# Loading a band of bias factors by DMA, loading a first q, k pair unpacked, and one DVE reordering, in a fused attention and maxout kernel

## The chip, the cores and the metric

The kernel runs on one core of one Trainium2 chip. The metric is the device time of one execution in microseconds (us); less is better. Engines are named as in the profile: PE is TensorE, ACT ScalarE, DVE VectorE, POOL GpSimd, SP SyncE. POOL, SP and ACT also issue DMAs.

## The reference

Inputs are q, k, v of shape (8, 8, 576, 64) (batch, heads, sequence, head dimension), a bias table of 32 buckets by 8 heads and four weight matrices, all float32. Cut to what matters:

```python
scores = q @ k.transpose(0, 1, 3, 2) / sqrt(D)
n = abs(pos[:, None] - pos[None, :])
scores += bias_table[bucket(n)].transpose(2, 0, 1)[None]   # constant for n >= 128 or so
attn = softmax(scores)                                     # over the keys
x = (attn @ v).transpose(0, 2, 1, 3).reshape(B * S, H * D) # 4608 tokens x 512
h = maximum(maximum(x @ w1, x @ w2), x @ w3)               # 768 wide
out = h @ w_out                                            # 4608 x 512, float32
```

## The kernel before, in words

Everything is computed in bf16 with float32 accumulation. The work goes batch by batch, and inside a batch by four pairs of heads (`hp` 0 to 3). For a pair PE makes transposed scores (keys on partitions, queries along the row), ACT takes their exponential into a tile `e4` for the first 512 keys and a tile `el` for the 64 left-over keys, PE multiplies by v with a column of ones behind it, and DVE divides by the row sums (`reciprocal`, then a product: the quotients, L962 and L963) into `x_sb`. Then `x_sb` is transposed into `xT` and fed to the three projections, of which chunks of 512 tokens (256 at the start) are laid between the attention work so that PE always has something to do.

The bias is not added to the scores. Its exponential, less a constant, is a factor that differs from 1 only in a band of 384 around the diagonal. `spread_bias` builds one row of 511 factors for each head and stores it to DRAM as `w_dr`. Two DMAs on SP's queue (`load_hank`, L340) read it back as `hank`: partition p holds the row shifted by p, 384 wide, 128x4x384 for each half of the heads. DVE multiplies the exponentials by reversed slices of `hank`: `times_band` (L807), `times_band_pair` (L822), `times_band_left` (L920). The left-over keys of a pair lie stacked, 64 partitions for each head, so they need another layout: `bandt`, 128 x 4 pairs x 192. In the kernel before, POOL makes it from `hank` with two reversing copies of 64x768 (`make_bandt`, L356), and `times_bandt` (L907) multiplies `el` by it.

Batch 0 (called batch one in the words of the change) is done in two passes. The first pass (loop at L1100) makes the scores of the first 256 queries of all four pairs, and at `hp` 3 DVE multiplies the bands of pairs 0 and 1. The second pass (loop at L1132) makes the other queries and meanwhile the first half of the values: at `hp` 0 the quotients of pair 0, then `bands(2)` (the bands of the third pair's first half), then the quotients of pair 1, then `bands(3)`; the copy of a transposed piece of q to `qT` (L126) comes behind. At `hp` 1 PE turns `x_sb` of pair 1 into `xT` (`x_transposes(1, 0)`, tiles `xp`), begins with the second half of the values, and so on. The second half of a pair's values (`attend(0, hp, e4, el, 1)`) reads the part of `el` that `times_bandt` writes.

Between the passes, `load_second` (L1072) puts on POOL's queue everything that batch 1 needs. q and k of batch 1 come packed: a partition takes four consecutive rows of a head, so that a run in DRAM and in the tile is long (`load_packed`, L247). They land in spare columns of `xT` and are spread into the tiles `q_sb`, `k_sb` (where the heads alternate) by `spread_packed` (L252): pair 0 by POOL, pairs 1 to 3 later by DVE. PE then transposes these (`second_transposes`, L781).

What sets the order: each engine runs its instructions in the order of the program (`inorder`). A DMA counts as an instruction of the engine that issues it, and POOL, SP and ACT issue in order too. DMAs of POOL use eight semaphores in turn (DMASW0 to DMASW7), so that one more DMA waits until the DMA eight before it has landed; DMAs of SP do the same with DMAHW0 to DMAHW7. `go_behind(loads, ins)` makes a load wait for an instruction `ins`. `divided[0, 0, 0]` is the second instruction (L963) of pair 0's first quotients. Tiles in PSUM come from pools with two buffers each (`ps_a` for the values, `ps_f` for transposes and projections, `ps_s` for scores).

## Time and profile before

| what | value |
|---|---|
| time, median of 3 runs | 308.22 us (306.51 to 308.97) |
| time of the profiled execution | 307.46 us |
| its span in the trace | 305.7 us |
| PE, DVE, ACT, POOL busy | 294.5, 206.9, 201.3, 143.7 us (96, 68, 66, 47%) |
| granted TensorE clock | 1.0 throughout |
| DMA, mean over the span | 133 GB/s in 165777 packets |

The span runs from the first to the last instruction; the time of the execution has 1.8 us around it. A row of the timeline gives the start, the length, the engine, the line, the operation with output <- inputs and, in brackets, how long the engine was idle before it and what ended that. Rows of the DMA view give the bytes of one DMA and the median time from its issue to its landing. A row of the DMA queues gives packets, MB and the time of the packets as a share of 16 DMA engines. Tile names in the profile have no numbers; in the order of instructions they do.

### The profile page before, as it was taken

To read this page: it belongs to the slowest core of one execution; us is meant where nothing else is said; L and a number is where in the kernel's file an instruction comes from. 1 tells how busy PE (TensorE), PEld (TensorE's weight loads), DVE (VectorE), ACT (ScalarE), POOL (GpSimd) and SP (SyncE) were. 2 spreads that over 40 slices of the span, in tenths; PEclk is the share of its full clock that TensorE was granted. 3 is DMA by queue.
4 is the path that set the end of the run, shared out by engine and by line. 5 is a ranking of instruction groups with operands and counts; after the bars stand their busy time and mean duration, and the time that the engine had idled before them with its cause. 6 is when DMAs were issued, how large, how long until landed. Compare 5 with 4: busy or idle time off the path is not lost.

```text
span 305.7 us, 10992 instructions
## 1 busy us (share of the span) xinstructions
PE 294.5 (96%) x4736; PEld 183.6 (60%) x4745; DVE 206.9 (68%) x455; ACT 201.3 (66%) x270; POOL 143.7 (47%) x199
## 2 busy tenths in 40 slices
PE   8778999999999999999999999999999999999995
PEld 2356878775556576667666766676667654444442
DVE  6489688787767767776777677767776765453552
ACT  3997998987786677768776877677777720222211
POOL 8998786725739655865686669460000000000000
PEclk9999999999999999999999999999999999999999
DMA  9999999999999999999999999999543013202003
GB/s 158 195 197 194 177 144 144 98 163 122 217 152 129 147 197 168 161 133 200 152 159 127 192 180 146 128 197 153 49 84 135 11 36 91 90 0 105 35 0 137
DMA packets 165777, 40.51 MB, mean 133 GB/s; under 512 B 154585, under 2 KB 161249, under 8 KB 165729
## 3 DMA queue, kind: packets, MB, share of 16 engines
q0 software_dynamic: 105664, 16.66, 96.6%
q1 hardware_dynamic: 58304, 22.69, 40.8%
q8 instruction: 37, 0.61, 0.9%
q10 hardware_dynamic: 1760, 0.47, 0.7%
q14 instruction: 12, 0.09, 0.2%
HBM read 35.39 MB, written 9.45 MB: 147 GB/s over the span
## 4 chain that ended last, share of the span: by engine, by line
PE 87%; ACT 6%; DVE 4%; issue 1%; DMA 1%; DVEq 0%; ACTq 0%
PE psp L109 36%; PE ps L109 17%; PE a L109 14%; PE sc L109 9%; PE pso L109 6%; ACT e L827 4%; PE sct L109 2%; PE warm L109 1%; PE scq L109 1%; DVE e L807 1%; ACT el L827 1%; DVE qT L126 1%; DMA out_dram<-osb 1%; DVE e L822 1%; PE tp L113 1%
## 5 line engine op out<-in xcount | busy, mean ns | idle before, releaser
L827 ACT ACTIVATE e<-sc 128x1024 bf16<-128x1024 f32 x128 | 129.0, 1026 | 29.6 <-PE sc L109 28.3
L109 PEld LDWEIGHTS <-w_bf 64*128 64x128 bf16 (+1 forms) x1112 | 75.9, 95 | 55.1 <-issue 1.5
L109 PE MATMUL psp<-xT,w_bf 64*128 64x512 bf16 x784 | 97.2, 376 | 0.0
L807 DVE TENSOR_TENSOR e<-e,hank 128x512 bf16<-128x512 bf16 (+2 forms) x120 | 57.7, 486 | 13.9 <-ACT e L827 13.2
L109 PE MATMUL ps<-xT,w_bf 128*128 128x512 bf16 (+1 forms) x324 | 58.9, 332 | 0.3
L109 PE MATMUL sc<-qT,kT 64*128 64x256 bf16 (+1 forms) x352 | 48.6, 319 | 2.4 <-ACT e L827 1.1
L199 POOL DMA_DIRECT2D k_sb<-in_k_dram x48 | 36.2, 768 | 18.3 <-DMA vx<-in_v_dram 10.6
L109 PE MATMUL a<-vx,e 64*128 64x65 bf16 (+1 forms) x1664 | 44.7, 190 | 0.0
L109 PEld LDWEIGHTS <-kT 64*128 64x128 bf16 (+1 forms) x712 | 30.1, 94 | 24.2 <-issue 7.1
L109 PEld LDWEIGHTS <-e 64*128 64x128 bf16 (+1 forms) x1664 | 40.7, 95 | 4.2
L199 POOL DMA_DIRECT2D q_sb<-in_q_dram x48 | 36.5, 771 | 11.9 <-DMA k_sb<-in_k_dram 3.0
L109 PEld LDWEIGHTS <-hT 64*128 64x128 bf16 (+1 forms) x462 | 28.2, 95 | 18.7 <-DVE hT L551 1.6
L167 POOL DMA_DIRECT2D vx<-in_v_dram x28 | 24.9, 899 | 23.0 <-DMA vx<-in_v_dram 9.3
L109 PE MATMUL psp<-wo_bf,hT 64*128 64x256 bf16 (+1 forms) x360 | 31.7, 305 | 0.0
L421 ACT ACTIVATE m<-ps 128x512 bf16<-128x512 f32 x14 | 8.4, 597 | 34.3 <-PE ps L109 34.3
L109 PEld LDWEIGHTS <-el 64*128 64x128 bf16 (+1 forms) x676 | 26.4, 94 | 7.0 <-issue 4.4
L827 ACT ACTIVATE el<-sct 128x576 bf16<-128x576 f32 (+2 forms) x36 | 21.7, 605 | 13.1 <-PE sct L109 13.0
L109 PE MATMUL a<-vt,el 64*128 64x65 bf16 (+1 forms) x260 | 29.6, 198 | 0.2 <-DVE m L511 0.2
L551 DVE TENSOR_TENSOR hT<-psp,m 128x1024 bf16<-128x1024 f32 (+1 forms) x20 | 18.7, 956 | 8.2 <-PE psp L109 8.2
L109 PE MATMUL pso<-wo_bf,hT 128*128 128x512 bf16 (+2 forms) x98 | 21.2, 366 | 0.2
L430 DVE TENSOR_TENSOR m<-ps,m 128x512 bf16<-128x512 f32 x14 | 9.7, 692 | 17.0 <-PE ps L109 17.0
L537 DVE TENSOR_TENSOR m<-psp,m 128x1024 bf16<-128x1024 f32 x15 | 18.4, 1224 | 3.3 <-PE psp L109 3.1
(82 smaller groups left out, 291.7 us busy)
## 6 DMA issues: line engine op xcount, KB each, us to landing
out_dram<-osb SPq DMA_DIRECT2D x35, 256.0 KB, 4.1
vx<-in_v_dram POOLq DMA_DIRECT2D x28, 128.0 KB, 6.3
q_sb<-in_q_dram POOLq DMA_DIRECT2D x50, 64.0 KB, 5.0
k_sb<-in_k_dram POOLq DMA_DIRECT2D x48, 64.0 KB, 4.8
w_bf<-in_moe_w_dram POOLq DMA_DIRECT2D x2, 512.0 KB, 8.5
xT<-in_k_dram SPq DMA_DIRECT2D x6, 128.0 KB, 4.6
hank<-w_dr SPq DMA_DIRECT2D x2, 384.0 KB, 4.8
w_bf<-in_moe_w_dram POOLq DMA_DIRECT2D x1, 768.0 KB, 8.4
```

The costliest lines, as they stand in the source:

```text
L109: made = inorder(nc.tensor.matmul(*args, **kw))
L113: inorder(nc.tensor.transpose(*args))
L126: return inorder(nc.vector.tensor_copy(out_, in_))
L167: in_turn(b, nc.gpsimd.dma_start(out=dst[:, t, h0:h1, :], in_=x[:, t, h0:h1, :]), P * (h1 - h0))
L199: in_turn(b, nc.gpsimd.dma_start(out=dst[:, g, :, par, :], in_=part), KT * P)
L421: nc.scalar.activation(out=st[fb]["m0"][:], in_=ps0, func=ACTF.Copy)
L430: inorder(nc.vector.tensor_tensor(out=m[:], in0=ps1, in1=st[fb]["m0"][:], op=ALU.max))
L537: return lambda: inorder(nc.vector.tensor_tensor(out=m[0][:], in0=ps1(), in1=m[0][:], op=ALU.max,))
L551: inorder(nc.vector.tensor_tensor(out=out_[:, i : i + n], in0=ps2()[:, i : i + n], in1=m[0][:, i : i + n], op=ALU.max,))
L807: put(nc.vector.tensor_tensor(out=e4[:, t, :, lo:hi], in0=e4[:, t, :, lo:hi], in1=hank[:, 2 * hp : 2 * hp + 2, c0:c1][:, :, ::-1], op=ALU. ...
L822: inorder(nc.vector.tensor_tensor(out=e4[:, t : t + 2, :, lo : lo + n], in0=e4[:, t : t + 2, :, lo : lo + n], in1=band, op=ALU.mult,))
L827: made = nc.scalar.activation(out=out_, in_=in_, func=ACTF.Exp, scale=inv_sqrt_d)
```

## The change

Three things are changed, all in the stage of batch 0's second pass, 15 to 40 us into the span.

1. `make_bandt` is replaced by `load_bandt`: two DMAs on SP's queue read `bandt` from `w_dr`, unreversed, and `times_bandt` reads it reversed. Both loads wait for pair 0's first quotients.
2. `load_second` loads pair 0 of batch 1 straight into `k_sb` and `q_sb`, a DMA for each head (128x4x64), and the other six heads packed as before, now behind the second weight matrix. POOL's spreading of pair 0 goes.
3. `bands(2)` is put ahead of pair 0's quotients.

```diff
-    def make_bandt():
+    def load_bandt(behind):
         for par in range(2):
-            r = slice(64 * par, 64 * par + 64)
-            c = BAND // 2 - 64 * par
-            inorder(nc.gpsimd.tensor_copy(bandt[r, :, :], hank[r, par::2, c : c + 192][:, :, ::-1]))
+            load = inorder(nc.sync.dma_start(
+                out=bandt[64 * par : 64 * par + 64, :, :],
+                in_=bass.AP(
+                    tensor=w_dr.tensor, offset=w_dr.offset + par * WL + BAND // 2,
+                    ap=[[1, 64], [2 * WL, HP], [1, 192]],
+                ),
+            ))
+            go_behind([load], behind)
...
-            out=el[:, S - 192 : S], in0=el[:, S - 192 : S], in1=bandt[:, hp, :], op=ALU.mult
+            out=el[:, S - 192 : S], in0=el[:, S - 192 : S], in1=bandt[:, hp, :][:, ::-1], op=ALU.mult
...
     def load_second():
-        for h0, h1 in ((0, 2), (2, H)):
-            load_packed(k, h0, h1, k_1)
-            load_packed(q, h0, h1, q_1)
-            if h0 == 0:
-                load_q_tail(1)
-                load_tail(k, 1, 0, H, k_diag)
-                load_w(1)
-                make_bandt()
-        spread_packed(0, nc.gpsimd)
+        for src, dst in ((k, batch[1][1]), (q, batch[1][0])):
+            for h in range(2):
+                x = src[1, h, 0 : KT * P, :].rearrange("(p t) d -> p t d", t=KT)
+                inorder(nc.gpsimd.dma_start(out=dst[:, :, h, :], in_=x))
+        load_q_tail(1)
+        load_tail(k, 1, 0, H, k_diag)
+        load_w(1)
+        load_packed(k, 2, H, k_1)
+        load_packed(q, 2, H, q_1)
         load_v(1, 0, H)
         load_w(2)
...
         quotients = next_late()
+        if hp == 0:
+            bands(2)
         if hp < 2:
             quotients()
             if hp == 0:
-                bands(2)
+                load_bandt(divided[0, 0, 0])
```

DVE in the second pass at `hp` 0, before. `a_390` and `a_432` are the values of pairs 0 and 1, `e4_289` and `e4_318` the exponentials of pairs 2 and 3, `tp2_456` the transposed piece of q.

```order
L126 COPY qT_189<-tp2_376 128x320 [waits PE_49]
L962 RECIPROCAL rd_409<-a_390 128x4 [waits PE_49]
L963 TENSOR_TENSOR x_sb_223<-a_390,rd_409 128x2x128 [waits DVE_49]
L822 TENSOR_TENSOR e4_289<-e4_289,hank_187 128x4x256 [waits DMAHW6_49,Activation_49]
L807 TENSOR_TENSOR e4_289<-e4_289,hank_187 128x2x128 [waits Activation_49]
L962 RECIPROCAL rd_451<-a_432 128x4 [waits PE_49]
L963 TENSOR_TENSOR x_sb_223<-a_432,rd_451 128x2x128 [waits DVE_49]
L822 TENSOR_TENSOR e4_318<-e4_318,hank_187 128x4x256 [waits Activation_49]
L807 TENSOR_TENSOR e4_318<-e4_318,hank_187 128x2x128 [waits Activation_49]
L126 COPY qT_189<-tp2_456 128x320 [waits PE_49]
```

The same place with the change:

```order
L126 COPY qT_189<-tp2_374 128x320 [waits PE_49]
L827 TENSOR_TENSOR e4_289<-e4_289,hank_187 128x4x256 [waits DMAHW6_49,Activation_49]
L812 TENSOR_TENSOR e4_289<-e4_289,hank_187 128x2x128 [waits Activation_49]
L967 RECIPROCAL rd_409<-a_388 128x4 [waits PE_49]
L968 TENSOR_TENSOR x_sb_223<-a_388,rd_409 128x2x128 [waits DVE_49]
L967 RECIPROCAL rd_451<-a_432 128x4 [waits PE_49]
L968 TENSOR_TENSOR x_sb_223<-a_432,rd_451 128x2x128 [waits DVE_49]
L827 TENSOR_TENSOR e4_318<-e4_318,hank_187 128x4x256 [waits Activation_49]
L812 TENSOR_TENSOR e4_318<-e4_318,hank_187 128x2x128 [waits Activation_49]
L126 COPY qT_189<-tp2_456 128x320 [waits PE_49]
```

The two band products of pair 2 have moved ahead of pair 0's quotients; nothing else on DVE has moved. The lines are five higher because the new loader is longer.

A little further on DVE, with the change, at the first use of `bandt` (`el_367` is pair 0's tile of left-over keys, `a_471` the values of pair 2):

```order
L967 RECIPROCAL rd_490<-a_471 128x4 [waits PE_49]
L968 TENSOR_TENSOR x_sb_223<-a_471,rd_490 128x2x128 [waits DVE_49]
L812 TENSOR_TENSOR e4_366<-e4_366,hank_187 128x2x128 [waits Activation_49]
L827 TENSOR_TENSOR e4_366<-e4_366,hank_187 128x4x256 [waits Activation_49]
L912 TENSOR_TENSOR el_367<-el_367,bandt_188 128x192 [waits DMAHW7_49,DMAHW0_49,Activation_49]
L925 TENSOR_TENSOR el_367<-el_367,hank_187 128x128 [waits Activation_49]
```

The product with `bandt` stands where it stood (L907 before), but where it waited for POOL it now waits for the two DMAs on SP's queue.

POOL from the first weight matrix (`w0_bf`) on, before. `xT_101` is where the packed q and k land, `w1_bf` the second weight matrix.

```order
L1066 DMA w0_bf_216<-in_moe_w1_dram 128x4x768 [waits DMASW2_49]
L247 DMA xT_101<-in_k_dram 128x2x256 [waits DMAHW2_49,DMAHW3_49,DMAHW1_49,DMAHW4_49,DMAHW0_49,DMAHW6_49,DMASW3_49,DVE_49]
L247 DMA xT_101<-in_q_dram 128x2x256 [waits DMASW4_49]
L177 DMA qtail1_98<-in_q_dram 64x8x64 [waits DMASW5_49]
L188 DMA ktail1_100<-in_k_dram 64x4x64 [waits DMASW6_49]
L188 DMA ktail1_100<-in_k_dram 64x4x64 [waits DMASW7_49]
L1066 DMA w1_bf_217<-in_moe_w2_dram 128x4x256 [waits DMASW0_49]
L1066 DMA w1_bf_217<-in_moe_w2_dram 128x4x512 [waits DMASW1_49]
L356 COPY bandt_188<-hank_187 64x768 [waits DMAHW6_49,DMAHW5_49]
L356 COPY bandt_188<-hank_187 64x768 [waits Pool_49]
L247 DMA xT_101<-in_k_dram 128x6x256 [waits DMASW2_49]
L247 DMA xT_101<-in_q_dram 128x6x256 [waits DMAHW7_49,DMASW3_49,Activation_49]
```

And with the change:

```order
L1071 DMA w0_bf_216<-in_moe_w1_dram 128x4x768 [waits DMASW2_49]
L1081 DMA k_sb_221<-in_k_dram 128x4x64 [waits DMASW3_49]
L1081 DMA k_sb_221<-in_k_dram 128x4x64 [waits DMASW4_49]
L1081 DMA q_sb_220<-in_q_dram 128x4x64 [waits DMASW5_49]
L1081 DMA q_sb_220<-in_q_dram 128x4x64 [waits DMASW6_49]
L177 DMA qtail1_98<-in_q_dram 64x8x64 [waits DMASW7_49]
L188 DMA ktail1_100<-in_k_dram 64x4x64 [waits DMASW0_49,DVE_49]
L188 DMA ktail1_100<-in_k_dram 64x4x64 [waits DMASW1_49]
L1071 DMA w1_bf_217<-in_moe_w2_dram 128x4x256 [waits DMASW2_49]
L1071 DMA w1_bf_217<-in_moe_w2_dram 128x4x512 [waits DMASW3_49]
L247 DMA xT_101<-in_k_dram 128x6x256 [waits DMAHW2_49,DMAHW3_49,DMAHW1_49,DMAHW4_49,DMAHW0_49,DMAHW6_49,DMASW4_49,DVE_49]
L247 DMA xT_101<-in_q_dram 128x6x256 [waits DMAHW5_49,DMAHW7_49,DMASW5_49,Activation_49]
```

Four DMAs stand where two were, so the DMA that waits for `w0_bf` (DMASW2) is now the first half of `w1_bf`; before, it was the packed load of the other six heads of k. Behind these rows the kernel before has POOL's two spreading copies (L252); with the change POOL has no copies left in this stage. SP issues the two loads of `bandt` between those of `hank` and the first transposes of batch 2.

## The prediction

> **What bounds the kernel now.** I read the page first, then a table of busy time in stretches of 4 us around the edited stage, then PE's waits and the timelines of PE, DVE, ACT and POOL there, then the DMAs. The page and the table (length, then busy us and instruction count of PE, PEld, DVE, ACT, POOL, then clock, DMA share, GB/s):
>
> ```profile
> PE 294.5 (96%) x4736; PEld 183.6 (60%) x4745; DVE 206.9 (68%) x455; ACT 201.3 (66%) x270; POOL 143.7 (47%) x199
> ```
>
> ```profile
> 16.00:20.00 4.00, 2.90 (x60) 2.16 (x56) 2.54 (x8) 3.95 (x7) 3.83 (x7) 1.00 1.77 179
> 20.00:24.00 4.00, 2.31 (x53) 1.82 (x50) 3.93 (x9) 2.79 (x6) 3.15 (x5) 1.00 1.42 193
> 24.00:28.00 4.00, 3.67 (x75) 2.55 (x71) 3.93 (x14) 3.41 (x7) 3.87 (x6) 1.00 1.41 202
> 28.00:32.00 4.00, 4.00 (x66) 3.27 (x63) 3.11 (x9) 4.00 (x9) 3.71 (x5) 1.00 1.45 193
> ```
>
> PE is the bound, and from 28 us on it is full. What can be won in the edited stage is idle time of PE between 16 and 28 us: 12 less 8.88, 3.1 us at the very most. ACT is full in the first row (3.95) and DVE, not ACT, in the second (3.93 against 2.79), so it is the second row that a relieved DVE can shorten. PE's largest wait of the stage is there too, in its timeline:
>
> ```profile
> 19.79 0.40 PE L109 MATMUL a<-vx,e 128*128 128x65 bf16 x8
> 21.80 0.29 PE L109 MATMUL scq<-qT,kT 64*128 64x64 bf16 x8 [0.16 <-ACT e L827]
> 23.62 0.27 PE L113 MATMUL xp<-ident,x_sb 128*128 128x128 bf16 x2 [1.53 <-DVE qT L126]
> 25.35 0.23 PE L109 MATMUL a<-vt,el 128*128 128x130 bf16 x1
> 25.66 0.22 PE L109 MATMUL a<-vt,el 128*128 128x130 bf16 x1
> 26.26 0.30 PE L109 MATMUL sct<-qT,kT 128*128 128x320 bf16 x1
> ```
>
> PE stands from 22.09 to 23.62 because `xp` needs the PSUM buffer that DVE's copy to `qT` empties. DVE and POOL at that place:
>
> ```profile
> 16.29 0.69 DVE L822 TENSOR_TENSOR e<-e,hank 128x1024 bf16<-128x1024 bf16 x1
> 16.89 0.28 DVE L807 TENSOR_TENSOR e<-e,hank 128x256 bf16<-128x256 bf16 x1
> 18.78 0.18 DVE L962 RECIPROCAL rd<-a 128x4 f32<-128x4 f32 x1 [1.37 <-PE a L109]
> 19.00 0.42 DVE L963 TENSOR_TENSOR x_sb<-a,rd 128x256 bf16<-128x256 f32 x1
> 20.09 0.91 DVE L807 TENSOR_TENSOR e<-e,hank 128x256 bf16<-128x256 bf16 x1
> 21.47 1.03 DVE L822 TENSOR_TENSOR e<-e,hank 128x1024 bf16<-128x1024 bf16 x1
> 22.43 0.91 DVE L807 TENSOR_TENSOR e<-e,hank 128x256 bf16<-128x256 bf16 x1
> 23.26 0.31 DVE L126 COPY qT<-tp 128x320 bf16<-128x320 bf16 x1
> 24.84 0.25 DVE L907 TENSOR_TENSOR el<-el,bandt 128x192 bf16<-128x192 bf16 x1
> ```
>
> ```profile
> 15.28 0.82 POOL L1066 DMA_DIRECT2D w_bf<-in_moe_w_dram  x1
> 21.07 2.13 POOL L356 COPY bandt<-hank 64x768 bf16<-64x768 bf16 x2
> 23.99 0.83 POOL L247 DMA_DIRECT2D xT<-in_k_dram  x1 [0.79 <-DMA xT<-in_k_dram]
> ```
>
> Beside POOL's copies the same DVE products take longer: 0.91 for 0.28 twice, 1.03 for 0.69 once, together 1.6 us more. The first of the three lies ahead of the copies' start, but starts on POOL are rough, and nothing else on POOL reads `hank`.
>
> **The bands ahead of the quotients.** `bands(2)` is a 0.69 and a 0.28 us product, 0.9 us when they follow each other. DVE is free from 17.41 to 18.78 there (1.37 us of idle time in its row), so it ends at 18.35 and costs nothing. If the second half of `hank` were late, it would push the quotients; `hank` is priced below (it landed at about 17), and the cover is 0.4 us. Pair 1's quotients no longer wait behind it and start when PE has its values (its row at 19.79), at about 20.15. Uncovered, the two products would cost their 0.9 us.
>
> **No copies on POOL.** With the products back at 0.69 and 0.28, DVE's chain is: quotients of pair 1 to 20.8, `bands(3)` to 21.6, the `qT` copy to 21.9 instead of 23.57, ahead of 22.09. So the wait of 1.53 us goes as a whole; scores before 22.09 are held by ACT and stay. ACT can take the gain:
>
> ```profile
> 22.23 0.62 ACT L827 ACTIVATE el<-scq 128x512 bf16<-128x512 f32 x1
> 23.93 0.38 ACT L123 ACTIVATE xT<-xp 128x256 bf16<-128x256 bf16 x1 [1.09 <-PE xp L113]
> 24.86 1.94 ACT L827 ACTIVATE e<-sc 128x1024 bf16<-128x1024 f32 x2 [0.54 <-PE sc L109]
> ```
>
> It is done at 22.85, copies `xp` until 23.2 and gets its scores at 23.33, 1.53 before 24.86. Behind that it has no more than 0.1 us of slack, so nothing larger can come of this wait. POOL's two spreading copies go too; what they cost DVE lies behind the place where `bandt` decides, and I give it nothing. Reading `bandt` reversed costs nothing: the 128x192 product at 0.25 lies between the reversed 128x256 at 0.28 and shorter ones.
>
> **The load of `bandt`, and what waits for it.** This is the term against the change. The loads wait for the quotient that ends at 19.42, so SP issues them at about 19.45. DVE, earlier now by 1.7 us, comes to the product with `bandt` at 23.15, and PE needs that product at 25.66 less 1.53, 24.13 (its row `a<-vt,el`, the second tile, the first that reads those columns). Behind the stuck DVE product stand pair 3's quotients and the next `qT` copy; behind PE's tile stands `sct`, which ACT wants next. With a landing at L the product ends at L + 0.25, so the gain is 25.66 less (L + 0.28), at most 1.53. All of it stays while L is under 23.85; nothing is left at 25.38.
>
> The trace has no such load. Two rows bound it. The near one is `hank`, the same row of DRAM, four times the bytes, beside loads of v in short runs. The far one is a pair of transposes on the same queue that were issued while the output matrix was being loaded:
>
> ```profile
> 10.96 0.92 SPq L340 DMA_DIRECT2D hank<-w_dr  x2
> ```
>
> ```profile
> DMA to landing us min/median/max: 4.0/4.8/5.6
> ```
>
> ```profile
> 57.44 1.20 SPq L731 DMA_TRANSPOSE qT<-q_sb  x1
> 58.75 1.82 SPq L731 DMA_TRANSPOSE kT<-k_sb  x1
> ```
>
> ```profile
> 56.71 0.83 POOL L1086 DMA_DIRECT2D wo_bf<-in_moe_w_out_dram  x1
> ```
>
> ```profile
> wo_bf<-in_moe_w_out_dram POOLq DMA_DIRECT2D x1, 768.0 KB, 9.4
> qT<-q_sb SPq DMA_TRANSPOSE x1, 9.1
> kT<-k_sb SPq DMA_TRANSPOSE x1, 8.8
> w_bf<-in_moe_w_dram POOLq DMA_DIRECT2D x1, 768.0 KB, 8.4
> ```
>
> `hank`'s two loads took 4.0 and 5.6 us, so that the second landed at about 17, ahead of 17.41. By 4.0 us, L is 23.5. By the transposes' 9.1 it is 28.5. Nearest is the second case: when `bandt` is issued, the first weight matrix, also 768 KB, is in flight (issued 15.28, landed 8.4 later at 23.7). The transposes landed at 66.5 and 67.5, that is 0.4 and 1.4 us after the matrix in front of them (56.71 + 9.4 = 66.1). The same behind 23.7 gives 24.1 and 25.1; the two `bandt` loads are smaller, so I take L = 24.7. The gain is then 25.66 - 24.98 = 0.7 us.
>
> **The q, k pair loaded straight, and what moves on POOL's queue.** Four DMAs in runs of 128 bytes replace two in long runs. Rates of the queue on POOL in two stretches of 1 us, with short runs and inside the weight matrix:
>
> ```profile
> q0 software_dynamic: 1108, 0.14, 217.4%
> q0 software_dynamic: 136, 0.21, 115.0%
> ```
>
> The pair's 256 KB are 2048 runs: 2048/1108 = 1.85 us for 0.256/0.21 = 1.2 us before, 0.6 more. `bandt`'s 0.19 MB add 0.9. So everything behind lands about 1.5 us later. The first half of the second weight matrix takes over the wait for the first (until 23.99, where the packed k stood); behind the first (23.7) the queues then hold 1.85 and 0.9 us of these loads, 1 us of q's and k's tails (1024 short runs) and 1.2 us of its own 256 KB: it lands at about 28.7. PE wants it at 32.21 less the gain:
>
> ```profile
> 32.21 1.04 PE L109 MATMUL ps<-xT,w_bf 128*128 128x256 bf16 x8
> ```
>
>  So that costs nothing. POOL issues nothing later than before: the copies it loses (2.1 us of them in the row above) cover the two added issues (0.8 each). The nearest place where PE meets a delayed transfer is the output matrix: landed at 66.1, first used here:
>
> ```profile
> 68.25 1.03 PE L109 MATMUL pso<-wo_bf,hT 128*128 128x512 bf16 x3
> ```
>
> The slack is 2.15 us. A delay of 1.5 and PE earlier by 0.7 use 2.2 of it, so it just about holds: 0 here, up to 0.9 in the full-gain case.
>
> **The sum.** 1.53 removed, 0.85 lost again to the late `bandt`, 0 to 0.1 at the output matrix: 0.7 us. The profiled execution (307.46, span 305.7) would go to 306.8, its span to 305.0. It stands 0.8 below the median of the runs, 308.22, so I predict a median of 307.5.
>
> **The rivals.** *Full gain:* `bandt` lands by 23.85. For it speaks `hank` at 4.0 us in a busy queue; against it the transposes that landed only after the matrix. The gain is 1.5 less up to a few tenths: 306.7 to 306.9. The Trainium skill (DMA: Bandwidth & Descriptors, "Queues, rings and completion order") says that a DMA engine goes round between the queues that have work, one packet at a time, so that a load on SP's queue would not have to wait for a whole matrix on POOL's; by that rule this rival wins. `hank` agrees, the transposes at 57.44 do not.
>
> *Given back:* the gain of the stage is real but PE then stands at the output matrix (or later for the transposes of `xT`) because all transfers are later. Decides when delay and gain exceed 2.15 us together; at a delay of 2.1 nothing is left: 308.2. For it: POOL's queue is busy without a gap from 15 us on, and POOL waits for landings. Against it: my delay is 1.5.
>
> *Slower:* `bandt` fares like the transposes in full and lands 9.1 us after its issue, at 28.5. PE then has its tile at 28.8 instead of 25.66: 3.1 us lost, 311.3. It decides from L = 25.4 on, with 1 us lost for each us. Against it: the matrix in front was issued 4 us earlier here, not 0.7.
>
> *Much more:* the stage is relieved of nearly all idle time of PE (3.1 us), 305.1. Against it: PE's waits for ACT in the same stage are not touched, 0.8 of the 3.1 us in one of them:
>
> ```profile
> PE sct L109 <- ACT e L827: 0.8, 1, 0.8
> ```
>
> **How the numbers follow.** The forecast (gain 0.4 to 1.1) has 0.42, full gain 0.25, given back (within 0.4 of before) 0.18, slower 0.10, much more 0.05. One per cent is 3.1 us and about what a measurement of this kernel can tell from no change (the runs of before spread over 2.5 us). Only *much more* helped by spread goes beyond it on the fast side, 0.07 with some of the full gain; of *slower* the upper end, 0.05; the rest, 0.88, is within 1%. The range holds forecast, full gain and given back with the spread of a median, and about half of slower: 305.7 to 309.2.
>
> **What would show it.** Right: no POOL copy after 16 us; DVE's L812 and L827 at 0.28 and 0.69 everywhere; PE's wait before `xp` gone or under 0.2; `bands(2)` ending before 18.5; a new wait of DVE at L912 of about 1.5 us, ended by the `bandt` load, and of PE at the second `a<-vt,el` tile; `bandt` landing 4.5 to 6 us after issue; `pso` starting near 67.6. Wrong: `bandt` landing within 4.4 us (full gain) or after 25.4 (slower), L812 still at 0.9 with no copies on POOL, or a wait of PE for `wo_bf`.

## The result and the profile after

| kernel | median of its runs | profiled execution | its span | granted clock |
|---|---|---|---|---|
| before | 307.68 us (306.25 to 308.97, 17 runs) | 307.46 us | 305.7 us | 1.0 |
| after | 309.86 us (309.08 to 312.59, 17 runs) | 310.47 us | 308.7 us | 0.989 |

The ratio after to before is 1.0078, 95% interval 1.0056 to 1.0099: the change makes the kernel 2.2 us slower, a small loss that is clear of the noise. The forecast of 307.5 us had the wrong sign and the median lies 0.7 us above the range.

Up to the first use of `bandt` the changed kernel does what was forecast. DVE's timeline of after:

```profile
17.58 0.69 DVE L827 TENSOR_TENSOR e<-e,hank 128x1024 bf16<-128x1024 bf16 x1
18.18 0.29 DVE L812 TENSOR_TENSOR e<-e,hank 128x256 bf16<-128x256 bf16 x1
...
21.30 0.32 DVE L126 COPY qT<-tp 128x320 bf16<-128x320 bf16 x1
...
22.28 0.69 DVE L827 TENSOR_TENSOR e<-e,hank 128x1024 bf16<-128x1024 bf16 x1
26.15 0.26 DVE L912 TENSOR_TENSOR el<-el,bandt 128x192 bf16<-128x192 bf16 x1 [3.18 <-DMA bandt<-w_dr]
```

The moved bands end at 18.47, in what was DVE's idle time; the products with `hank` take 0.29 and 0.69; the `qT` copy ends at 21.62 instead of 23.57. Then DVE stands for 3.18 us for the load. PE's timeline of after:

```profile
21.74 0.28 PE L113 MATMUL xp<-ident,x_sb 128*128 128x128 bf16 x2
...
26.46 0.29 PE L109 MATMUL a<-vt,el 128*128 128x130 bf16 x1 [2.51 <-DVE el L912]
...
31.41 1.69 PE L109 MATMUL ps<-xT,w_bf 128*128 128x256 bf16 x8
...
33.78 0.93 PE L109 MATMUL ps<-xT,w_bf 128*128 128x256 bf16 x7
```

The row of `xp` has no bracket any more: the wait of 1.53 us is gone. In its place PE waits 2.51 us at the tile that needs `bandt`. That tile starts at 26.46 where it started at 25.66, so 0.8 us are lost there. But the lag keeps growing behind it, without any wait. The same two groups of `ps` in PE's timeline of before:

```profile
29.06 1.04 PE L109 MATMUL ps<-xT,w_bf 128*128 128x256 bf16 x8
...
30.78 1.03 PE L109 MATMUL ps<-xT,w_bf 128*128 128x256 bf16 x8
```

The lag is 2.35 us at the first (31.41 less 29.06) and 3.00 at the second, and the first group takes 1.69 us for 1.04. The cause is in the table by stretches of after, in the third column from the end, the granted clock (columns as in the prediction):

```profile
20.00:24.00 4.00, 3.78 (x75) 2.68 (x73) 2.90 (x9) 3.73 (x8) 2.53 (x4) 1.00 1.62 183
24.00:28.00 4.00, 1.54 (x23) 1.24 (x25) 1.82 (x7) 0.93 (x2) 3.75 (x6) 0.74 1.59 180
28.00:32.00 4.00, 4.00 (x51) 3.03 (x51) 2.53 (x11) 3.35 (x6) 3.53 (x5) 0.50 1.36 200
32.00:36.00 4.00, 3.95 (x45) 3.11 (x42) 1.81 (x4) 2.87 (x7) 1.50 (x2) 0.91 1.99 172
```

The clock is 0.74, 0.50 and 0.91 where before had 1.00. The shortfall is 4 x (0.26 + 0.50 + 0.09) = 3.4 us of full clock, that is 6.8 us at half. PE had been idle for about 2 us when it fell (0.96 in 25 to 26 us, 0.50 from 26 on). The account of the profiled execution is therefore 0.8 us for the late tile and 2.2 us, the rest, for matmuls at half speed; the 3.0 us stay to the end (span 308.7 against 305.7). Over the 17 runs the granted clock of a whole run is either 0.989 (6 runs, median 310.5 us) or 0.993 to 0.995 (11 runs, median 309.7): the shortfall of the profiled run (3.4 of 308.7 us gives 0.989), or half of it.

Why the load is late shows in SP's timeline, in the DMA issues between 15 and 27 us and in the DMA queues of two stretches of 1 us, 22 to 23 and 24 to 25 (q0 is POOL's queue, q1 carries SP's loads: packets, MB, share of 16 engines), all of after:

```profile
19.16 1.34 SPq L354 DMA_DIRECT2D bandt<-w_dr  x2
```

```profile
w_bf<-in_moe_w_dram POOLq DMA_DIRECT2D x1, 768.0 KB, 7.9
```

```profile
q0 software_dynamic: 971, 0.16, 210.0%
q1 hardware_dynamic: 4, 0.00, 0.9%
```

```profile
q0 software_dynamic: 637, 0.08, 122.8%
q1 hardware_dynamic: 259, 0.09, 55.0%
```

`bandt` was issued at 19.2 to 20.5. In 20 to 22 us q1 moves no packet at all and in 22 to 23 four, while the first weight matrix (issued at 15.23, landed 7.9 later at 23.1) and the pair's short runs go through q0. From 23 to 26 it gets its 540 packets beside 637 to 739 a us of q0, and DVE goes on at 26.15, some 7 us after the first issue. The first of these packets moves at 22.8 to 23.0, 3.7 us after the issue; those of `hank` in the kernel before moved 1.3 us after theirs (10.96, first packets at 12.2 to 12.4).

### The profile page after: what moved, and what is told of

It reads as the page before. It is cut to its first block, busy times and chain, and to the rows that moved or that the text cites. A ratio compares the mean times of both kernels' runs of the same rounds, so it can differ in the third digit from the quotient of the medians.

```text
span 308.7 us, 10992 instructions
## 1 busy us (share of the span) xinstructions
PE 297.0 (96%) x4736; PEld 185.3 (60%) x4745; DVE 205.4 (67%) x455; ACT 201.5 (65%) x270; POOL 142.0 (46%) x197
## 4 chain that ended last, share of the span: by engine, by line
PE 85%; DMA 5%; ACT 4%; DVE 3%; issue 1%; SPq 0%; DVEq 0%; ACTq 0%
PE psp L109 36%; PE ps L109 16%; PE a L109 14%; PE sc L109 8%; PE pso L109 6%; PE sct L109 2%; DMA bandt<-w_dr 2%; ACT e L832 2%; DMA hank<-w_dr 2%; PE warm L109 1%; DMA w_dr<-w_sb 1%; PE scq L109 1%; ACT el L832 1%; DMA out_dram<-osb 1%; DVE e L827 1%
## 5 line engine op out<-in xcount | busy, mean ns | idle before, releaser
L812 DVE TENSOR_TENSOR e<-e,hank 128x512 bf16<-128x512 bf16 (+2 forms) x120 | 56.2, 473 | 13.9 <-ACT e L832 13.2
L109 PE MATMUL a<-vx,e 64*128 64x65 bf16 (+1 forms) x1664 | 45.7, 191 | 0.0
L109 PEld LDWEIGHTS <-e 64*128 64x128 bf16 (+1 forms) x1664 | 41.5, 95 | 4.3
```

The lines of the kernel that those rows point to most:

```text
L109: made = inorder(nc.tensor.matmul(*args, **kw))
L812: put(nc.vector.tensor_tensor(out=e4[:, t, :, lo:hi], in0=e4[:, t, :, lo:hi], in1=hank[:, 2 * hp : 2 * hp + 2, c0:c1][:, :, ::-1], op=ALU. ...
```

## The experiments

All were timed in five rounds beside the kernel before. A lag is the start of an instruction less that of the same instruction in the profiled run before; it is worked out for one instruction each from the timelines of ACT and DVE, at the place where before stands at the time on top:

```
                     15.25  34.13  59.38  84.91 106.09 128.06 298.10   ratio to before [95%]
after                -0.30   3.00   3.02   3.02   3.02   3.17   3.17   1.0078 [1.0056, 1.0099]
e1_bandt_early       -0.01  -1.60  -0.05  -0.05  -0.06   0.61   0.85   1.0045 [1.0015, 1.0074]
e2_keep_busy          0.10   0.71   0.73   0.73   0.73   0.80   1.90   1.0123 [1.0082, 1.0163]
e3_packed_pair       -0.46   2.95   2.96   2.96   2.96   4.19   4.23   1.0128 [1.0103, 1.0152]
e4_bandt_by_pool     -0.39  -1.52  -0.91  -0.85  -0.85   0.17   0.37   1.0002 [0.9976, 1.0028]
e5_order_only        -0.54  -1.09  -1.08  -1.08  -1.08  -0.47  -0.46   0.9981 [0.9959, 1.0002]
e6_packed_early      -0.26  -1.85  -1.84  -1.29  -1.29   2.87   2.91   0.9997 [0.9972, 1.0023]
e7_weights_first     -0.42  -0.28  -0.27   0.03   0.03   0.03   0.36   1.0040 [1.0021, 1.0059]
e8_half_busy         -0.25   0.75   0.77   2.00   2.00   2.22   2.25   1.0065 [1.0043, 1.0088]
e9_packed_early_2    -0.01  -1.60  -1.59  -0.57  -0.57   0.35   0.36   0.9999 [0.9972, 1.0026]
e10_early_only       -0.08  -1.67  -1.65  -1.66  -1.65  -0.50  -0.21   1.0008 [0.9976, 1.0041]
e11_early_turned      0.05  -1.54  -1.53   5.62   5.62   6.00   6.01   1.0176 [1.0134, 1.0217]
e12_turn_only        -0.44  -1.56  -1.54   5.18   5.18   5.17   5.17   1.0123 [1.0073, 1.0173]
```

The first column is what a run happened to have ahead of the stage; the second less the first is what the stage gave. Two things limit this table. A profiled execution is one run and not the median: that of e6 is the slowest of its runs, those of e2 and e7 are the fastest of theirs. And what the stage gives differs between executions of the same program. e12 is the kernel before as far as 62 us, and yet its stage is 1.12 us shorter than the profiled one of before. PE's timeline of e12:

```profile
22.07 0.27 PE L113 MATMUL xp<-ident,x_sb 128*128 128x128 bf16 x2 [0.42 <-DVE qT L126]
```

The wait of 1.53 us ahead of `xp` is 0.42 here, with the old order and with POOL's copies. The trace lists the copies from 21.80 instead of 21.07, after POOL had waited 0.72 us for a piece of v, and two of the three DVE products that were slow in before take 0.28 us. So a gain of 1.6 us against the profiled run of before is 0.5 against this one, and how much the other runs of before lose here is not on record.

**e1: `bandt` loaded early.** In the changed kernel the two loads are issued right behind those of `hank` and wait for no quotient:

```diff
     for h0 in (0, KT):
         load_hank(h0, h0 + KT)
+    load_bandt(None)
...
             if hp == 0:
-                load_bandt(divided[0, 0, 0])
+                pass
```

> The changed kernel with one edit: the two loads of bandt are issued right behind those of hank, at about 11 us, and wait for no quotient. Theory (the whole loss comes from bandt landing late, as a PE wait and the half clock that follows it): bandt lands by 19, DVE does not wait at L912, PE does not wait at the second a<-vt,el tile, the clock stays at 1.0, and what is left is the gain of the rest: about 1.5 us below before, 306.2. Rival (the added short runs make every later transfer late, and that costs the time): the wait at L912 goes but the time stays above 309. Second rival (the early loads push the second half of hank or v): a new wait of 0.5 to 1 us between 16 and 20 us, 307.

Median 308.18 us against 307.22. No wait for `bandt`, clock 1.00, and the stage's gain is there in full: 1.6 us by the table. It is gone at 41 us. PE's timeline, POOL's, and the table by stretches of this kernel:

```profile
41.03 0.23 PE L109 MATMUL a<-vt,el 128*128 128x130 bf16 x1 [1.34 <-DMA vt<-in_v_dram]
42.22 1.05 PE L109 MATMUL ps<-xT,w_bf 128*128 128x256 bf16 x8 [0.18 <-DMA w_bf<-in_moe_w_dram]
```

```profile
25.15 1.50 POOL L1072 DMA_DIRECT2D w_bf<-in_moe_w_dram  x2 [2.94 <-DMA w_bf<-in_moe_w_dram]
```

```profile
24.00:28.00 4.00, 3.68 (x79) 2.93 (x76) 3.51 (x14) 3.95 (x8) 2.85 (x4) 1.00 1.17 88
```

PE meets v's tail and the third weight matrix, both late. POOL's issue of the second weight matrix, at 19.59 before, stood until 25.15 for the landing of the first: with four DMAs in place of two it is the eighth behind it, and POOL's eight semaphores go in turn. Meanwhile little was queued, and only 88 GB/s moved in 24 to 28 us where before moved 202. So the rival that the prediction called *given back* is real, 27 us ahead of the place where it was expected. The two loads of `bandt` took 6.5 and 7.1 us here too, behind those of `hank`; issued at 11.65, they were there in time.

**e2: PE kept busy while it waits.** The changed kernel with eleven matmuls on zeros in front of the waiting tile; their result is not used (the trace has ten of the eleven).

```diff
+            if (b, hp, half, i) == (0, 0, 1, 0):
+                on_zeros(ps_f.tile([P, CH], F32, tag="ff", name="idle")[:], 11)
```

> The changed kernel with eleven matmuls on zeros (128x512, results not used) put on PE just ahead of the tile that waits for bandt, so that PE works through most of the wait. The load is as late as in the changed kernel. Theory (of the 3.0 us that the trace loses, 0.8 is the wait itself and 2.2 the half clock behind it): the clock stays at 1.0 from 24 to 33 us, the wait of DVE at L912 is still 3 us, and the time falls by about 2 us, to 307.7 to 308.3. Rival (the clock falls for another reason than the idle time, or the slow matmuls only fill time in which DVE or ACT are the bound): the clock still falls, or the time stays at 309.5 or more.

PE's timeline and the table by stretches of this kernel:

```profile
24.18 2.54 PE L109 MATMUL idle<-xT 128*128 128x512 bf16 x10
26.62 0.23 PE L109 MATMUL a<-vt,el 128*128 128x130 bf16 x1
```

```profile
24.00:28.00 4.00, 3.95 (x50) 2.23 (x49) 1.66 (x7) 1.75 (x4) 3.39 (x5) 1.00 1.35 148
28.00:32.00 4.00, 3.91 (x62) 2.95 (x61) 3.82 (x13) 4.00 (x9) 3.88 (x5) 1.00 1.20 173
```

The tile starts at 26.62, as late as in after (26.46), but the clock stays at 1.00 and the lag at 34 us is 0.71 instead of 3.00. That shows that in this stage the 2.2 us behind the tile come from the clock. The time of the kernel does not follow: 310.14 us. In the profile another 1.1 us went at 140 us, where PE stands 0.9 us; the trace puts it down to an exponential of ACT that had ended 0.4 us before PE went on, so its cause is open.

**e3: the pair packed.** The changed kernel with the second part undone: pair 0 of batch 1 packed, and spread by POOL.

```diff
-        for src, dst in ((k, batch[1][1]), (q, batch[1][0])):
-            for h in range(2):
-                x = src[1, h, 0 : KT * P, :].rearrange("(p t) d -> p t d", t=KT)
-                inorder(nc.gpsimd.dma_start(out=dst[:, :, h, :], in_=x))
-        load_q_tail(1)
-        load_tail(k, 1, 0, H, k_diag)
-        load_w(1)
-        load_packed(k, 2, H, k_1)
-        load_packed(q, 2, H, q_1)
+        for h0, h1 in ((0, 2), (2, H)):
+            load_packed(k, h0, h1, k_1)
+            load_packed(q, h0, h1, q_1)
+            if h0 == 0:
+                load_q_tail(1)
+                load_tail(k, 1, 0, H, k_diag)
+                load_w(1)
+        spread_packed(0, nc.gpsimd)
```

> The changed kernel with its second part undone: the first pair of batch 1 comes packed as before and POOL spreads it; bandt still by DMA behind the first quotients. Theory (the bandt loads wait for every load that POOL had issued before them, the weight matrix and the pair's short runs alike): the pair now has a quarter of the packets, bandt lands about 1 to 1.5 us earlier, near 24.8, PE's wait falls to about 1.2 us, too short to lower the clock; time 307.0 to 307.7. Rival (only the weight matrix holds bandt back): landing near 26 as in the changed kernel, clock at half, 309.5 to 310.

PE's timeline of this kernel at the tile that waits:

```profile
26.77 0.29 PE L109 MATMUL a<-vt,el 128*128 128x130 bf16 x1 [3.00 <-DVE el L912]
```

311.47 us. The load is as late as in after: DVE goes on at 26.14 (26.15 there). The wait is longer, not shorter, because the product with `bandt` now takes 0.57 us instead of 0.26, beside POOL's spreading copies (from 25.43), and PE had come 0.2 us earlier. The clock falls as in after (0.69, 0.50 and 0.96 in the three stretches from 24 us). My theory that the pair's short runs hold `bandt` back has fallen; the rival, that the weight matrix ahead of it does, stands, but no run issues the load at this place without the matrix, so it is argued and not shown.

**e4: `bandt` by POOL's copies again.** The changed kernel with the first part undone; the copies stand ahead of the second weight matrix.

```diff
         load_q_tail(1)
         load_tail(k, 1, 0, H, k_diag)
+        make_bandt()
         load_w(1)
...
             if hp == 0:
-                load_bandt(divided[0, 0, 0])
+                pass
```

> The changed kernel with its first part undone: POOL makes bandt from hank with its two copies, put behind the tails of k and ahead of the second weight matrix (at about 22 us); pair straight and bands(2) ahead as in the change. Theory: without the late load nothing of the loss is left; the copies slow DVE's products beside them by some tenths and bandt is there at about 24, near the time PE wants it: 306.5 to 307.5. Rival (the straight pair costs the time): 309 or more.

307.45 us against 307.22, as expected. With the copies back and the other two parts kept, the loss of 2.2 us is gone, so of the three parts it is the load of `bandt` that makes the kernel slower; loading it early (e1, 1.0045) takes back only a part of that. The stage gives 1.1 us, and PE's timeline has 0.6 of it lost at the same two places as in e1, with a further 1.0 us lost between 106 and 128 us:

```profile
40.03 0.23 PE L109 MATMUL a<-vt,el 128*128 128x130 bf16 x1 [0.34 <-DMA vt<-in_v_dram]
41.32 1.05 PE L109 MATMUL ps<-xT,w_bf 128*128 128x256 bf16 x8 [0.27 <-DMA w_bf<-in_moe_w_dram]
```

**e5: the order alone.** The kernel before with `bands(2)` ahead of the first quotients.

```diff
+        if hp == 0:
+            bands(2)
         if hp < 2:
             quotients()
             if hp == 0:
-                bands(2)
+                pass
```

> The kernel before with one edit: the third pair's bands ahead of the first pair's quotients; GpSimd still copies bandt, the pair stays packed. My theory (the order of DVE's chain and POOL's copies share the gain): bands of pair 3 end at about 18.5 in DVE's idle time, the next bands still meet the copies (0.91 and 1.03 instead of 0.28 and 0.69), so the qT copy ends at about 22.8 instead of 23.57, PE's wait ahead of xp shrinks from 1.53 to about 0.7 us, and all 0.8 us is kept: 306.4 where before has 307.2. No late load, so no drop of the clock. Rival (the gain comes from the copies alone): the wait stays at 1.5, time as before.

306.79 us against 307.61. PE's timeline of this kernel, and a row of DVE's:

```profile
22.04 0.27 PE L113 MATMUL xp<-ident,x_sb 128*128 128x128 bf16 x2 [0.49 <-DVE qT L126]
```

```profile
20.85 0.91 DVE L807 TENSOR_TENSOR e<-e,hank 128x256 bf16<-128x256 bf16 x1
```

PE's wait is 0.49 us instead of 1.53 while one product, just ahead of the copies (listed from 22.10), still takes 0.91. The stage gives 0.55 us (0.8 expected), kept as far as 106 us; 0.42 us are lost at 24.1, where PE waits for a product beside the copies. But e12 has a wait of 0.42 us with the bands in their old place, and its copies too are later than in before. So this run does not show that the order shortened the wait; the later copies do as well. Its ratio is the lowest of all kernels here, but its interval reaches 1: no difference from before is shown.

**e10: the early load alone.** The kernel before with `bandt` loaded right behind `hank`; order and pair as before.

```diff
     for h0 in (0, KT):
         load_hank(h0, h0 + KT)
+    load_bandt(None)
...
                 load_w(1)
-                make_bandt()
```

> The kernel before with one edit: bandt comes by DMA right behind the load of hank instead of GpSimd's copies; the bands keep their place behind the first quotients and the pair stays packed. My theory (the copies' contention with DVE alone makes PE's wait ahead of xp): DVE's products are at 0.28 and 0.69, the qT copy ends at about 22.0, PE's wait ahead of xp is 0 to 0.2 us, and the lag against before is -1.4 to -1.6 us at 30 to 60 us, so that the moved bands add nothing to it. Rival (the order sets it): the wait stays at 0.7 us or more and the lag is -0.8 or less.

DVE's timeline, and PE's, of this kernel:

```profile
20.77 0.68 DVE L827 TENSOR_TENSOR e<-e,hank 128x1024 bf16<-128x1024 bf16 x1
21.37 0.28 DVE L812 TENSOR_TENSOR e<-e,hank 128x256 bf16<-128x256 bf16 x1
21.57 0.32 DVE L126 COPY qT<-tp 128x320 bf16<-128x320 bf16 x1
```

```profile
21.95 0.28 PE L113 MATMUL xp<-ident,x_sb 128*128 128x128 bf16 x2
...
119.55 0.39 PE L109 MATMUL sc<-qT,kT 64*128 64x512 bf16 x2 [0.97 <-DMA kT<-k_sb]
```

And SP's:

```profile
111.18 1.26 SPq L736 DMA_TRANSPOSE kT<-k_sb  x1
```

Without the copies the products are at 0.28 and 0.68 and PE's wait is gone: 1.6 us against the profiled run of before (0.5 against e12) from this alone, and the moved bands add nothing to it (e6 and e9 have 1.6 too). The Trainium skill (SBUF — State Buffer, "Who interferes with whom") says that a DVE instruction with two SBUF inputs contends with a GpSimd instruction that reads SBUF; the 0.91 and 0.28 of the same product, with and without copies, agree. Yet the time is that of before: 307.38 against 307.35. The gain is there as far as 106 us and 1.15 of it go between 106 and 128, where PE waits 1.0 us for a transposed `kT` that SP issued at 111.18. It landed 8.3 us later, at 119.5. In before the same load was issued at 111.08 and landed at 119.5 as well, and PE came at 120.05: the transfer is no earlier, so PE, being earlier, waits for it.

**e6 and e9: early load, moved bands, packed pair,** the same program twice. The edit, against e3:

```diff
     for h0 in (0, KT):
         load_hank(h0, h0 + KT)
+    load_bandt(None)
...
             if hp == 0:
-                load_bandt(divided[0, 0, 0])
+                pass
```

> Parts one and three without part two: bandt comes by DMA right behind the load of hank, waiting for nothing; the bands are moved; the first q, k pair of batch two stays packed and is spread by GpSimd. My theory (the gain of 1.5 us in the stage is real, and it was given back in the kernel with the early load because the straight pair made the second weight matrix wait for the first one's landing): the second weight matrix is issued by 21.5 as before, the DMA queue moves about 200 GB/s in 24 to 28 us, no wait of DVE for bandt, no wait of PE for vt or w_bf at 40 to 43, clock 1.00, and 305.7 to 306.0 where before has 307.2, span 304.2. Rival (GpSimd's spreading, or the 192 KB of bandt, delays the transfers just as much): waits at 40 to 45 as with the straight pair, 307 to 308.

> The same program as the one with the early load of bandt, the moved bands and the packed pair, looked at a second time: its first profile kept 1.85 us until 78 us and lost 4.7 us at 78 and 113 to 119, where PE met a transposed kT of batch two 2.4 us late and the clock fell, while its runs ranged from 306.2 to 310.2. My theory (the gain of the edited stage is always there, and what varies is where the transposes of batch two land): the same -1.6 to -1.9 us against before from 30 to 75 us, a wait of PE at 78 or 113 of another size than 2.4, and runs spread over 3 us or more around 307. Rival (the late transposes belong to this order of loads): the wait at 113 comes again at 2 us or more, and so does the drop of the clock.

307.61 us against 307.61, and 307.39 against 307.35; single runs from 305.9 to 310.2. PE's timeline and the table by stretches in e6, then PE's timeline in e9:

```profile
113.56 0.39 PE L109 MATMUL sc<-qT,kT 64*128 64x512 bf16 x2 [2.42 <-DMA kT<-k_sb]
```

```profile
112.00:116.00 4.00, 2.44 (x62) 1.86 (x63) 1.18 (x3) 1.02 (x1) 2.10 (x3) 0.84 1.69 250
116.00:120.00 4.00, 4.00 (x72) 2.56 (x68) 1.92 (x5) 1.91 (x3) 1.59 (x3) 0.73 1.88 193
```

```profile
112.60 0.39 PE L109 MATMUL sc<-qT,kT 64*128 64x512 bf16 x2 [0.74 <-DMA kT<-k_sb]
```

Both carry the 1.6 us to 60 us. Both lose it at 78 us (0.5 and 1.0) and at the `kT` of 112 us, by 2.42 and 0.74; the rival that its size is fixed falls. In e6 the wait of 2.42 lowers the clock once more (shortfall 4 x (0.16 + 0.27) = 1.7 us, 3.4 us at half). So the time won at 22 us is not lost in the stage: PE arrives earlier at transfers that do not come earlier. Here they even came later: SP issued the `kT` of 112 us at 108.67 in e6 and 108.04 in e9, in before at 105.34; why is open. That these waits take the gain is shown for the profiled runs; for the others it is inferred from the medians. These also fit the other reading, that most runs of before lose less than 1.53 us at 22 us, as e12 does.

**e7: the second weight matrix ahead of the straight q.** This is e1 with the two straight q loads behind `load_w(1)`.

```diff
         pair(k, batch[1][1])
         load_q_tail(1)
         load_tail(k, 1, 0, H, k_diag)
         load_w(1)
+        pair(q, batch[1][0])
```

> The kernel with the early load of bandt, but the two straight q loads of the pair are issued behind the second weight matrix instead of ahead of it, so that only five DMAs stand between the two matrices' first halves. My theory (the eighth DMA behind the first matrix waits for its landing): the second matrix is issued by 21 without a wait, and the wait for the first matrix's landing moves to the straight q loads at about 24 to 25; the DMA queue no longer runs dry at 25 to 28, the waits of PE for vt and w_bf at 40 to 43 (1.5 us) go, time 306 to 306.5. Rival (the later issues behind the wait are what counts, not the dry queue): k and q of the other pairs are issued at 26 as before, and the waits at 40 to 43 stay at 1 us or more: 307.7 to 308.2.

308.67 us against 307.61. The table by stretches and PE's timeline of this kernel:

```profile
24.00:28.00 4.00, 3.68 (x79) 2.93 (x76) 3.51 (x14) 3.95 (x8) 2.97 (x4) 1.00 1.46 194
```

```profile
31.38 0.38 PE L113 MATMUL tp<-ident,q_sb 128*128 128x128 bf16 x4 [1.16 <-DMA q_sb<-in_q_dram]
```

The queue no longer runs dry (194 GB/s for 88), but the wait for the first matrix now holds q back, and PE loses 1.16 us at 31 us. The waits at 40 to 43 are gone (the lag is -0.28 at 34 us and -0.27 at 59), but PE comes there 1.3 us later than in e1, so this run does not tell whether the dry queue or the later issues made them.

**e8: half of the wait filled.** Against e2:

```diff
-                on_zeros(ps_f.tile([P, CH], F32, tag="ff", name="idle")[:], 11)
+                on_zeros(ps_f.tile([P, CH], F32, tag="ff", name="idle")[:], 6)
```

> The changed kernel with six products on zeros instead of eleven ahead of the tile that waits: they keep TensorE busy for about 1.4 us of its wait and leave it idle for about 1.2 us, less than the 1.53 that did not lower the clock in the kernel before. My theory (what lowers the clock is the length of the idle time): clock 1.00 throughout, the lag against before is 0.7 to 0.9 at 33 us and stays, 308.0 to 308.3 where before has 307.2 and the changed kernel would have 309.5. Rival (the clock falls by how much work lies in a stretch, so that 1.2 us is enough): half clock for 3 to 6 us, 309 to 310.

PE's timeline, and the table by stretches, of this kernel:

```profile
23.83 1.46 PE L109 MATMUL idle<-xT 128*128 128x512 bf16 x6
26.66 0.23 PE L109 MATMUL a<-vt,el 128*128 128x130 bf16 x1 [1.37 <-DVE el L912]
```

```profile
28.00:32.00 4.00, 3.90 (x63) 2.91 (x61) 3.86 (x13) 4.00 (x9) 3.98 (x6) 1.00 1.28 191
```

With 1.37 us idle the clock stays at 1.00 and the lag at 34 us is 0.75, as expected. The time is 309.9 us, not 308.2: in the profile 0.34 us go between 68 and 72 us (0.17 of it a wait for the output matrix) and 0.9 at 79 us. So e2 and e8 show the clock's share within the stage, but without it the run is as long as after: what is won goes to waits further on. Its price for the whole kernel, taken alone, is not shown.

**e11 and e12: a later pair of transposing loads issued earlier,** with e10 and with the kernel before. The edit changes a list of places:

```diff
-    places = {2: ((1, 1, 0), (1, 1, 1), (1, 2, 0), (1, 3, 1), (2, 1, 0)), 3: ((2, 2, 0), (2, 2, 1), (2, 3, 0), (3, 0, 0), (3, 0, 1))}
+    places = {2: ((1, 1, 0), (1, 1, 1), (1, 2, 0), (1, 3, 1), (2, 0, 1)), 3: ((2, 2, 0), (2, 2, 1), (2, 3, 0), (3, 0, 0), (3, 0, 1))}
```

> The kernel with only bandt loaded early (bands in their old place, pair packed), and one more edit far behind: the transposing loads of q and k of the fourth pair of the third batch, which SP issues at 103 to 107 us behind the five transposes of x_sb, are issued between the second and third of those. My theory (the 1.6 us won at 22 us reaches that place and is spent there, because kT of that pair lands at 111 to 113 whatever PE does): kT is issued at about 102 instead of 106, the wait of PE for it (1.0 us in the kernel with the early load) is gone, the lag against before stays at -1.3 to -1.7 us from 30 us to the end, span 304.2, and the median is 306.0 where before has 307.4. Rival (the whole stretch is bound by its transfers, so the wait moves to the next one, the transposed x_sb or the following pair): 307 to 307.5, with a wait of PE of 0.7 us or more at another load between 105 and 125 us.

> The kernel before with only that later pair of transposing loads issued earlier, bandt by GpSimd's copies as before. My theory: nothing is won at 22 us; in the profiled run before PE did not wait for that kT, so the median is within 0.4 us of before, 307.0 to 307.5. Rival (the late kT takes time of most runs of before as well, and its profile was a lucky one): 0.6 us or more below before.

312.44 and 310.53 us against 307.35. I had the wrong pair: the edit moved the one that SP issues at 72 us, into the transposes of `x_sb` at 63 to 72, and left the later ones where they were. (The load that made PE wait in e10 was not the one at 103 to 107 either, but the one at 111.18.) So neither expectation was tested. What it did, in PE's timeline and the stretches of e11:

```profile
79.89 1.89 PE L109 MATMUL psp<-xT,w_bf 64*128 64x512 bf16 x8 [4.35 <-DMA xT<-x_sb]
```

```profile
76.00:80.00 4.00, 0.11 (x2) 0.14 (x4) 0.84 (x2) 0.61 (x1) 3.21 (x5) 0.81 1.52 149
80.00:84.00 4.00, 4.00 (x30) 1.92 (x29) 0.26 (x2) 0.60 (x1) 3.58 (x5) 0.50 1.54 229
84.00:88.00 4.00, 4.00 (x47) 2.26 (x44) 2.40 (x6) 3.10 (x5) 1.50 (x2) 0.84 2.08 158
```

SP, which issues in order, stood for q and k of the moved pair to land, and the other three transposes of `x_sb` left at 74.6 to 79.0 (before: all five by 71.7). PE stands 4.35 us for them; the clock falls again, with a shortfall of 3.4 us. In e12 PE stands 4.28 us at the same place, and the shortfall is 1.7 us (4 x 0.43, with 0.57 in 80 to 84 us and 1.00 around it).

## Why the prediction was wrong

- **The wait of 1.53 us, the bands and the copies: right.** All of it went. e10 shows that the end of the copies is enough; what the moved bands are worth alone is not shown (e5 beside e12). But I took the 1.53 from one execution as if it were the kernel's: in e12 the same wait is 0.42, so the removed term is 0.4 us in one run and 1.5 in the other.
- **The landing of `bandt`: the term that was mis-sized.** I took 24.7, one of two landings of a pair of transposes behind another matrix, shortened because the loads are smaller. It was 26.1. The matrix landed at 23.1, 0.6 earlier than I assumed, but the load then took 3 us more: before 22.8 it had moved nothing, and from there it shared the engines. The formula held: 25.66 less (26.15 + 0.28) is a loss of 0.77, measured 0.8. By it the median would have been 309.0 us (307.5 + 0.7 + 0.8), or 308.5 from the 307.68 of 17 runs, still inside the range. The sign I had named for this case, a landing after 25.4, is what the profile shows.
- **"1 us lost for each us" in the rival *slower*: the step that failed.** That rival was the right mechanism, with a chance of 0.10. But its price left out what PE's idle time does to PE itself. I had counted idle time as idle time; it also bought 6.8 us at half clock, 2.2 us in the profiled run. The wait of 1.53 us in before, at a clock of 1.00, had told nothing of it. With this term the same landing gives 310.4 (307.46 + 0.77 + 2.2), where the profiled execution took 310.47; as the 2.2 is read from the same trace, that is no test of it. The test is e2, in which the clock stays and the lag is 0.71 us instead of 3.00. For the median it is less clear: e2 and e8 keep the clock and, by waits further on, are no faster than after, so of the 2.2 us by which the median rose the clock's share is open. That all of it hangs on the load of `bandt` is shown by e4.
- **The rule of the round between the queues** (the Trainium skill, DMA: Bandwidth & Descriptors, "Queues, rings and completion order"): by it *full gain* would have won. The trace does not agree for 20 to 23 us, in which q1 had 192 KB waiting and moved four packets; from 23 us on it got its share.
- **Part two at 0 us: not so.** I saw that the second weight matrix takes over the wait for the first and checked only its own landing. "POOL issues nothing later than before" was wrong: in after the second matrix is issued at 23.37 instead of 19.59, the third at 32.96 instead of 32.10. In e1 this wait leaves the queue dry, and v's tail and the third matrix, which follow on the same queue, are what PE meets at 41 us. In after it stays hidden behind a PE that is 3 us late.
- **Where the stage's gain goes: half seen.** *Given back* named the output matrix at 68 us with 2.15 us of slack. PE did stand at the output matrix, 0.72 us in e12, where it came early, and 0.17 us in e8. The other places were 41 us (with the straight pair), 78, 112 and 119 us.

## What to carry to other kernels

Price a new wait by its landing time and by what it does to the clock: in this kernel PE idle for 1.4 to 1.5 us cost just that, and idle for 2.4 us or more cost up to 2.2 us on top. Do not cost a load that is issued beside a large transfer in flight on another queue by one that was not: here it moved its first packets 3.7 us after its issue instead of 1.3, and landed 3 us after that transfer. Issue it earlier, where it can wait for nothing. Before a wait read from one profile goes into a sum, look at it in a second one. And a gain in one stage is worth nothing until the next transfers that PE meets have been checked: follow the lag through the whole trace rather than stop at the edited stage.

## What the runs showed of the hardware

- **The clock falls in units.** PE idle for 2.42 us (e6), 2.51 (after), 3.00 (e3) and 4.35 (e11) was followed by half clock; 1.37 (e8) and 1.53 (before) was not. The shortfall was 1.7 us of full clock in e6 and 3.4 in the other three, that is 3.4 or 6.8 us at half; but 4.28 us in e12 brought only 1.7, so the length of the wait does not set the number of units. Nor does the fall come at a fixed point of the wait: in after about 2 us into it, in e6 more than 1 us after PE had gone on at 113.56 (0.87 in 114 to 115 us, 0.50 from 115 on). The Trainium skill (TensorE: Matmul & The Clock Gate, "Part 1: The HAM clock gate") has a free-running window of 3.4 us for this; the lengths agree, and so does a fall that is not tied to the start of the wait. It asks for an idle window of about 3.4 us; here 2.4 us of idle time was enough.
- **A waiting queue can get next to nothing for 3 us** beside large loads of another queue (the 4 packets of q1 above). From issue to first packet, `bandt` took 3.7 us in after and 3.8 in e3, and the transposes issued at 57.44 in before 4.2; `hank` took 1.3. Those transposes moved their first packets at 61.6 us, 4.5 us before the matrix beside them landed (66.1), so it is not simply the other transfer's landing that a queue waits for.
- **POOL's eighth DMA back is a wait.** Two more DMAs between two large ones moved POOL's wait from the packed k to the second matrix, and in e1 the queue ran dry: 88 GB/s for 202 in before.
